# Gated SSM and squared-ReLU layer, forward and backward, on one core: the first dense layer by feature blocks ahead of the periods, its results loaded back and squared by ScalarE

## The chip, the core and the metric

The kernel runs on one core of a Trainium2 chip. Its engines are named as the profile names them: PE (TensorE matmul, with PEld for its weight loads), DVE (VectorE), ACT (ScalarE), POOL (GpSimd) and SP (SyncE). ACT, POOL and SP also issue transfers; a wait ahead of an issue is shown as SPq, ACTq or POOLq. Each engine works through its own instructions in the order in which they stand in the program, and semaphores hold an instruction until what it reads or overwrites is ready. The metric is the device time of one execution in microseconds (us).

## What is computed

The reference is the value and the gradients of one function. Cut to what matters here:

```
g = sigmoid((x * gate_w).sum(-1))
a = irfft(rfft(u) * rfft(K)) + u * Dskip          # K from A, B, C, log_dt (448 features, 256 states)
h = x @ w1 + b1                                   # 2048 x 448 @ 448 x 1792
r = where(h > 0, h, 0)
b = (r * r) @ w2 + b2                             # 1792 -> 448
out = g * a + (1 - g) * b
_out, _vjp = jax.vjp(f, ...); _grads = _vjp(grad_out)
```

The backward pass of the dense part needs r again: the gradient at h is 2 * r * (db @ w2.T), and the gradients of w1 and w2 read that product and the square of r. In both kernels r is therefore also written to memory (tensor `rT_d`, feature-major, 1792 x 2048).

## The kernel before, in words

The program has five parts, one after the other.

1. Start: loads, the gate, a first transform (`fwd1`) and transposes; `UT` (in tile `S25`, the variable `SB`) receives the transposed input, which is the moving operand of the first dense layer.
2. FFT stage: `powers` (a chain of squarings that ACT and DVE hand to each other, DVE L592 and L593, ACT L582 and L591), `spectra` (`load_s1`, `fwd2`), `products` (DVE L288) and `inv1` (PE L303), whose result goes to memory as `hd`. In parts 1 and 2 a scheduler decides the order of each engine's instructions from the dependencies; from part 3 on (`tc.manual_schedule()`) they stand as written.
3. Handover: `hd` is loaded back by SP (L312). DVE builds the tables of chunk 0 and then of chunk 1 (`tables`, `tables_y`), ACT first spreading each chunk's record over the table fields (`fields_x`, `fields_y`, L709 to L720). PE sums the convolution's rows with 116 matmuls (L1037); ACT copies the six results out (L1044); they go to memory (`dk_d`) and come back as `DK`; ACT copies transposed tables (L790), scales (L796), and copies out the first kernel chunk (L760).
4. Thirteen periods, one per chunk c = 1 to 13. The string `PERIOD` lists the tokens of a period; each builds the tables of chunk c and works backward on chunk c - 1. Ten of its tokens are `D`: at each, `D_` runs some steps of the generator `dense()`, so that the dense layers are spread evenly over the periods. The copy L760 stands near the end of each period and marks it in a trace.
5. Tail: the remaining rows of chunk 13, the second transform back, the parameter gradients, and the gradients of w1 and w2 (`units`, called by `Fl`).

The dense part before: `first_layer` goes through four token blocks (lb) of 512 and, in each, seven feature pairs (jp) of 2 x 128. One such step, an **h step** in what follows, is eight PE matmuls of 512 columns (six of 128 rows at L905, two of 64 rows at L908), two Relu on ACT out of two PSUM banks (L912), a write of r to memory by POOL (L913), and one square on DVE (L915, two steps late by `later`) into `hblk`. After the seven steps of a block `project` multiplies `hblk` with w2 in eight half steps (PE L883, ACT copy L887). At the last block the transposes of w1 (`turn_w1`, ACT copy L941) stand beside it, then those of w2 (`turn_w2`, L951). `second_layer` follows: per step matmuls, two scalings on ACT (L968) and one product with r, loaded back, on DVE (L971). Period 1 takes 8 of the 127 steps (`first_steps`), each later period 119/12. The square and the product are the dense part's only work on DVE.

All of w1 is loaded by SP in the handover (L1020, L1022). r has four buffers by turns (`rx`). The tables of chunks up to 6 are turned by four transposing transfers on SP (`load_yt`, L779); from chunk 7 on (`ON_PE`) the fourth is done by PE with two ACT copies (L790, R<-psN).

## Time and profile before

| | |
|---|---|
| runs | 805.06, 808.89 and 812.79 us, median 808.89 |
| the profiled execution's own time | 813.03 us |
| its span, first to last instruction | 811.2 us |
| busy PE / DVE / ACT / POOL | 621.9 / 612.7 / 539.4 / 162.0 us |
| granted TensorE clock, mean | 0.871 |
| end of each period (start of L760) | 257.9, 285.7, 311.0, 338.4, 363.9, 392.7, 418.8, 442.5, 469.6, 494.5, 519.7, 546.0, 568.7 us |
| start of period 1 (L760 of chunk 0) | 229.6 us |

Busy times overlap: they are shares of one span. A row of the windows view gives, for a stretch of the span, the busy time of each engine with the number of instructions, then the granted clock (1.00 is full speed), the DMA share and GB/s. A row of the timeline gives start, duration, engine, line, what it writes and reads, and in brackets how long the engine had sat idle and for whom it waited. Rows of the grouped lines end with the total busy time, the mean of one in ns, and the idle time before it.

### The profile page before, as it was taken

What the parts mean: (1) busy time and instruction counts of PE and PEld (TensorE: products, weight loads), DVE (VectorE), ACT (ScalarE), POOL (GpSimd) and SP (SyncE); (2) the same over time, 40 slices, a digit from 0 to 9 for tenths busy, and PEclk for the clock granted to TensorE, in tenths of its full rate; (3) what the DMA queues carried; (4) which work ended last, traced back from release to release, by engine and by line L of the source; (5) the groups of instructions that cost most, each with busy time, mean ns of one, the idle gap of its engine ahead of it and who ended that gap; (6) DMA issues with size and microseconds to landing.
All of it is one profiled execution on the core that took longest, in us unless ns stands there. A gap on an engine that the chain in (4) does not pass through costs nothing. (4 is left out here: it accounts for less than half of the span.)

```text
span 811.2 us, 17087 instructions
## 1 busy us (share of the span) xinstructions
PE 621.9 (77%) x6845; PEld 303.0 (37%) x6845; DVE 612.7 (76%) x947; ACT 539.4 (66%) x879; POOL 162.0 (20%) x264
## 2 busy tenths in 40 slices
PE   3776367663378889988989889989778689898985
PEld 1222122121243334434554444534535234444442
DVE  3795597877834999989789989989657864888263
ACT  0696467670578687968899879884575487465463
POOL 1222000042111132213231001101135311123122
PEclk9986555565688989999989999999989899999998
DMA  9978766279759387968986979895689998999972
GB/s 192 240 204 282 298 244 233 90 286 212 211 109 186 76 198 142 200 124 217 196 158 112 290 175 228 176 246 139 207 274 311 368 294 289 285 301 330 255 218 63
DMA packets 167214, 175.73 MB, mean 217 GB/s; under 512 B 104068, under 2 KB 144990, under 8 KB 166542
## 3 DMA queue, kind: packets, MB, share of 16 engines
q1 hardware_dynamic: 140152, 97.89, 49.9%
q0 software_dynamic: 17552, 56.44, 22.8%
q10 hardware_dynamic: 9430, 20.31, 7.2%
q8 instruction: 53, 0.87, 0.5%
q14 instruction: 27, 0.22, 0.1%
HBM read 83.67 MB, written 67.53 MB: 186 GB/s over the span
## 5 line engine op out<-in xcount | busy, mean ns | idle before, releaser
L817 ACT CAST P<-psF 128x1024 bf16<-128x1024 f32 x56 | 57.2, 1021 | 27.8 <-PE psF L815 27.7
L656 DVE TENSOR_TENSOR F<-X,F 128x1024 bf16<-128x1024 bf16 (+2 forms) x42 | 64.4, 1533 | 9.8 <-ACT X L689 7.3
L883 PEld LDWEIGHTS <-U 128*128 128x128 bf16 x448 | 40.9, 100 | 48.0 <-issue 16.6
L883 PE MATMUL psN<-D,U 128*128 128x448 bf16 x224 | 54.1, 386 | 1.1 <-DMA D<-in_B_w_dram 0.7
L888 POOL DMA_DIRECT2D br_d<-D x32 | 17.5, 548 | 180.0 <-ACT D L887 173.7
L1201 PEld LDWEIGHTS <-S 128*128 128x128 bf16 x416 | 39.0, 99 | 38.6 <-issue 9.3
L1201 PE MATMUL psX<-D,S 128*128 128x449 bf16 x224 | 47.2, 353 | 1.7 <-ACT S L1207 1.5
L883 PE MATMUL psN<-S,U 128*128 128x448 bf16 x224 | 46.8, 353 | 1.5 <-issue 1.3
L963 PE MATMUL psN<-S,K 128*128 128x512 bf16 x168 | 42.4, 386 | 6.0 <-ACT R L790 5.6
L815 PE MATMUL psF<-R,S 41*32 41x256 bf16 x896 | 24.7, 291 | 28.0 <-DVE P L828 17.4
L827 DVE TENSOR_TENSOR M<-P,psF 128x2048 bf16<-128x2048 bf16 x28 | 34.1, 1216 | 14.0 <-PE psF L773 12.5
L905 PE MATMUL psN<-S,K 128*128 128x512 bf16 x168 | 43.1, 395 | 0.0
L1201 PE MATMUL psX<-K,S 128*128 128x448 bf16 x192 | 41.2, 359 | 1.7 <-ACT S L1204 1.7
L1192 ACT ACTIVATE S<-psN 128x1024 bf16<-128x1024 bf16 x32 | 33.0, 1030 | 13.7 <-PE psN L1188 13.6
L303 PE MATMUL psN<-D,cb_MI 64*128 64x448 bf16 x96 | 31.7, 532 | 9.1 <-DVE D L288 5.5
L303 PEld LDWEIGHTS <-cb_MI 64*128 64x128 bf16 x256 | 17.6, 110 | 53.2 <-issue 46.5
L265 PEld LDWEIGHTS <-M 128*64 128x64 bf16 x192 | 13.9, 133 | 62.6 <-issue 54.9
L657 DVE TENSOR_TENSOR X<-F 128x512 bf16<-128x512 bf16 (+2 forms) x42 | 35.6, 847 | 1.4
L968 ACT ACTIVATE U<-psN 128x512 bf16<-128x512 f32 x56 | 31.1, 616 | 7.6 <-PE psN L966 5.3
L796 ACT COPY S<-K 128x128 bf16<-128x128 bf16 x56 | 34.9, 1007 | 0.0
L828 DVE TENSOR_TENSOR P<-P,psF 128x2048 bf16<-128x2048 bf16 x28 | 34.2, 1221 | 1.0
L773 PE MATMUL psF<-ident,X 128*128 128x128 bf16 x448 | 31.8, 228 | 3.0 <-ACT P L817 2.9
(350 smaller groups left out, 1617.3 us busy)
## 6 DMA issues: line engine op xcount, KB each, us to landing
sp<-K ACTq DMA_DIRECT2D x8, 896.0 KB
dhT_d<-U SPq DMA_DIRECT2D x28, 256.0 KB
R<-sp SPq DMA_DIRECT2D x8, 896.0 KB
S<-dhT_d POOLq DMA_DIRECT2D x14, 512.0 KB, 7.3
R<-hd SPq DMA_DIRECT2D x16, 448.0 KB
S<-rT_d POOLq DMA_DIRECT2D x12, 512.0 KB, 7.0
hd<-st SPq DMA_DIRECT2D x13, 448.0 KB
rec<-rec_d POOLq DMA_DIRECT2D x11, 448.0 KB, 4.8
```

Of the source, the lines that this page charges most:

```text
L303: nc.tensor.matmul(ps[kk2][:, 0:D], lhsT=MI[r0:r0 + 64, m, :], rhs=rh[r0:r0 + 64], start=(k_ == 0), stop=(k_ == len(terms) - 1), tile_posi ...
L656: V.tensor_tensor(out=Vt[:, 0:2 * w * n], in0=run(lo, 0, [0, 2], [NA, w], [1, n]), in1=run(PX[:, 0:1], 512 * k, [2, w], [0, n], [1, 2]), o ...
L657: V.tensor_tensor(out=run(lo, n, [NA * X2, 2], [NA, X2], [1, n]), in0=run(vb, 0, [n * X2, 2], [n, X2], [1, n]), in1=run(vb, (w + X2) * n, ...
L796: S.copy(D2[:, :, 0, 4 * l:4 * l + 4].rearrange("p (g i) a -> p a g i", g=NG), DK[:, l::4].rearrange("p a (e g q i) -> p a e q g i", g=NG, ...
L817: S.copy(zbs[c, g // 2][:, :, g % 2].rearrange("p t h k n -> p t k h n"), psz[:].rearrange("p t (k h n) -> p t k h n", k=2, h=2))
L827: V.tensor_tensor(out=pr.rearrange("p t g h k n -> p t (g h k n)"), in0=zv, in1=xv, op=ALU.mult)
L828: V.tensor_tensor(out=zv, in0=zv, in1=rev_dim(xv, 1), op=ALU.mult)
L883: T_.matmul(ps[:, 0:D], lhsT=hblk[:, j, P * tt:P * tt + P], rhs=ws[:, j, :], start=(w == 1 and j == 0), stop=(j == FT - 1))
L905: T_.matmul(pss[k][:], lhsT=w1w[:, dt, j * P:j * P + P], rhs=UT[:, dt, 512 * lb:512 * lb + 512], start=(dt == 0), stop=False, skip_group_c ...
L963: T_.matmul(pss[k][:], lhsT=w2Tw[:, jp, dt, k], rhs=dblk[:, dt], start=(dt == 0), stop=False, skip_group_check=True)
L1192: S.activation(hn(i)[:, 8 * th:8 * th + 8, :], ps[:], ACT.Square if i < FT else ACT.Copy)
L1201: T_.matmul(ps[:, 0:w], lhsT=hn(i)[:, t, :], rhs=(DB2[:, t, :] if i < FT else U[:, t, 0:w]), start=(t == 0), stop=(t == LT - 1))
```

## The change

The 28 h steps are now taken feature pair by feature pair (jp outer, lb inner), and only the 256 columns of w1 that a pair needs are loaded (`load_w1b`, seven blocks, the first five on POOL in the FFT stage, two on SP in the handover). 16 h steps (pairs 0 to 3) stand in the FFT stage, with one Relu on ACT and one on DVE; 4 (pair 4) in the handover and 8 (pairs 5 and 6) in period 1, with both on ACT. In the FFT stage and the handover they use the two PSUM banks X and S. r is only written to memory. Its buffers are four in the FFT stage, three in the handover, and from `del hbuf[2:]` on two.

Whole w1, for its transposes, is loaded after period 1 (`behind`), and r is loaded back by SP into six buffers (`load_rx`) and squared by ACT (`square`), blocks by turns into `hvs[0]` and `hblkB`, where the lower half of `KW` serves as the second buffer after w1. The seven `turn_w1` and the squares of block 1 stand in the first projection; the squares of blocks 2 and 3 in the next two. `ON_PE` begins at chunk 2. DVE has no squares any more. Periods 2 to 13 take the remaining 102 of 111 steps.

```diff
+    HP = FT // 2
+    W1B = ct["Ew_tile"]
+    w1bs = [RA[:, 7168:8192], SB[:, 11264:12288], Pct_[:, 7168:8192], RA[:, 7168:8192], Pct_[:, 7168:8192], W1B[:, 4096:5120], W1B[:, 5120:6144]]
+    def load_w1b(jp, q_):
+        wb, f0 = w1bs[jp], 256 * jp
+        q_.dma_start(wb[:, 0:3], bass.AP(tensor=B_w1.tensor, offset=B_w1.offset + f0, ap=[[F, P], [P * F, 3], [1, 256]]))
...
+    hleft = [(jp, lb) for jp in range(HP) for lb in range(4)]
+    hbuf = [RA[:, 10752 + 1024 * i:11776 + 1024 * i] for i in range(3)] + [Fp[:, 7168:8192]]
+    hbanks = [lambda: K.ps("X", [P, 512]), lambda: K.ps("S", [P, 512])]
+    def h_step(bks, on_act):
+        jp, lb = hleft.pop(0)
...
+        for k in range(2):
+            b1 = b1_f[:, 2 * jp + k:2 * jp + k + 1]
+            if on_act[k]:
+                S.activation(r[:, 512 * k:512 * k + 512], pss[k][:], ACT.Relu, bias=b1)
+            else:
+                V.tensor_scalar(out=r[:, 512 * k:512 * k + 512], in0=pss[k][:], scalar1=b1, scalar2=0.0, op0=ALU.add, op1=ALU.max)
+        G_.dma_start(pair_rows(rT_d, jp, lb), r.rearrange("p (k l) -> p k l", k=2))
+    def H(n=1):
+        for _ in range(n):
+            h_step(hbanks, (True, False))
     for q in range(4):
         if q < 3:
             spectra(q + 1)
+        if q == 0:
+            for jp in range(3):
+                load_w1b(jp, G_)
...
+        H(2)
         for h in range(2):
             K.products(Pct[:, h], spw[:, 2 * (q % 2) + 1, 2 * h:2 * h + 2], spw[:, 2 * (q % 2), 2 * h:2 * h + 2])
             K.inv1(None, q, hd[0], (h,), Pct[:, h])
+            H(1)
...
+    def load_rx(i, q):
+        if i < 4 * HP:
+            q.dma_start(rx[i % 6].rearrange("p (k l) -> p k l", k=2), pair_rows(rT_d, i % HP, i // HP))
+    def square(i):
+        jp, lb = i % HP, i // HP
+        hb = hblkB if lb % 2 else hvs[0][:, 0:7168].rearrange("p (j l) -> p j l", j=FT)
+        S.activation(hb[:, 2 * jp:2 * jp + 2].rearrange("p k l -> p (k l)"), rx[i % 6], ACT.Square)
+        load_rx(i + 6, nc.sync)
     def first_layer():
-                def sq(jp=jp, r=r):
-                    V.tensor_tensor(out=hblk[:, 2 * jp:2 * jp + 2].rearrange("p k l -> p (k l)"), in0=r, in1=r, op=ALU.mult)
-                later(sq)
...
+        while hleft:
+            h_step([bank, bank], (True, True))
+            yield
...
+        rx.extend([SB[:, 6272 + 1024 * i:7296 + 1024 * i] for i in range(4)] + [hv[:, 7168:8192], st4])
+        for i in range(6):
+            behind.append(lambda i=i: load_rx(i, nc.sync))
+        behind.append(lambda: nc.sync.dma_start(w1w[:, 0:3], bass.AP(tensor=B_w1.tensor, offset=B_w1.offset, ap=[[F, P], [P * F, 3], [1, F]])))
...
+        for i in range(HP):
+            square(i)
+            if i % 2:
                 yield
+        def ex0(k):
+            for v in (2 * k, 2 * k + 1):
+                if v < HP:
+                    turn_w1(v)
+                elif 8 <= v < 8 + HP:
+                    square(HP + v - 8)
+        yield from project(0, 0, w2n, ex0)
+        for lb in (1, 2):
+            yield from project(lb, 0, w2n, lambda k, lb=lb: square(HP * lb + HP + k) if k < HP else None)
...
     tables_y(0)
-    nc.sync.dma_start(w1w[:, 0:3], bass.AP(tensor=B_w1.tensor, offset=B_w1.offset, ap=[[F, P], [P * F, 3], [1, F]]))
...
     tables_y(1)
+    del hbuf[:]
+    hbuf += [SB[:, 8192:9216], SB[:, 9216:10240], SB[:, 11264:12288]]
+    for _ in range(4):
+        h_step(hbanks, (True, True))
     psS = [K.ps(NT[i], [P, 512]) for i in range(4)]
...
+    del hbuf[2:]
...
-    ON_PE = range(7, NCH - 1)
+    ON_PE = range(2, NCH - 1)
```

The order of the instructions at the places that matter, engine by engine (names with a line of the program, the operation, what it writes and reads, and the size; M and F are the record of chunk 1 and the table fields, psX and psS the two banks, U the constant weights of the row sums, S the tile `S25`).

ACT in the handover, before, from the last field of chunk 0 to the copies of the row sums:

```order
L720 ACTIVATE F_181_1339<-rec_1343 128x6x64x2 x2
L709 COPY F_181_1339<-M_182_1340 128x2x3x128
L712 ACTIVATE F_181_1339<-M_182_1340 128x3x128 x2
L717 COPY F_181_1339<-M_182_1340 128x6x256
L720 ACTIVATE F_181_1339<-M_182_1340 128x6x64x2 x2
L1044 CAST st_1532<-psN_184_1411 128x448
```

The same place now:

```order
L773 ACTIVATE F_213_1562<-rec_1566 128x6x64x2 x2
L762 COPY F_213_1562<-M_214_1563 128x2x3x128
L765 ACTIVATE F_213_1562<-M_214_1563 128x3x128 x2
L770 COPY F_213_1562<-M_214_1563 128x6x256
L773 ACTIVATE F_213_1562<-M_214_1563 128x6x64x2 x2
L652 ACTIVATE S_8_163<-psX_1637,b_f 128x512
L652 ACTIVATE S_8_163<-psS_1638,b_f 128x512
L652 ACTIVATE S_8_163<-psX_1650,b_f 128x512
L652 ACTIVATE S_8_163<-psS_1651,b_f 128x512
```

The eight Relu of the four handover steps (four are shown) stand behind the fields of chunk 1 and ahead of the copies of the row sums.

PE at that place, before: the last matmul of the FFT stage is followed by the row sums.

```order
L303 LDWEIGHTS cb_MI
L303 MATMUL psN_175_1312<-D_89_656,cb_MI 128x448
L1037 LDWEIGHTS U_90_657
L1037 MATMUL psN_184_1411<-D_89_656,U_90_657 32x448
L1037 LDWEIGHTS U_90_657
```

Now, from the end of the fourth handover step:

```order
L643 MATMUL psS_1677<-S_8_163,D_89_656 128x512
L646 LDWEIGHTS D_89_656
L646 MATMUL psX_1676<-S_8_163,D_89_656 128x512
L646 LDWEIGHTS D_89_656
L646 MATMUL psS_1677<-S_8_163,D_89_656 128x512
L1123 LDWEIGHTS U_90_657
L1123 MATMUL psN_224_1689<-D_89_656,U_90_657 32x448
```

All four h steps stand ahead of the first row sum, and each takes banks X and S again.

SP from the record of chunk 1 to the transposing transfers of chunk 2, before:

```order
L701 DMA M_182_1340<-rec_d 128x1792
L1020 DMA K_177_1325<-in_B_w_dram 128x3x1792
L1022 DMA K_177_1325<-in_B_w_dram 64x1792 x2
L701 DMA rec_1639<-rec_d 128x1792
L779 DMA_TRANSPOSE R_178_1328<-R_178_1328 128x16x128 x4
L1159 DMA cb_F1BD<-c_F1K 128x256
L779 DMA_TRANSPOSE R_178_1328<-Y_179_1329 128x16x128 x4
```

And now, from the record of chunk 2 on:

```order
L754 DMA rec_1916<-rec_d 128x1792
L832 DMA_TRANSPOSE R_210_1551<-R_210_1551 128x16x128 x4
L963 DMA S_8_163<-rT_d 128x2x512 x4
L963 DMA U_269_2428<-rT_d 128x2x512
L963 DMA st_1834<-rT_d 128x2x512
L982 DMA K_209_1548<-in_B_w_dram 128x3x1792
L984 DMA K_209_1548<-in_B_w_dram 64x1792 x2
L963 DMA S_8_163<-rT_d 128x2x512 x4
```

The load of whole w1 (L982, L984) has moved behind the six first loads of r (L963), and each later load of r stands behind the square that frees its buffer.

More of the change, by code (lines that the diff above doesn't have):

```diff
@@ L871, in later, with project @@
             lates.pop(0)()
-    def project(lb, w, ws):
+    hvs = []
+    def project(lb, w, ws, extra=None):
+        hb = hblkB if w == 0 and lb % 2 else hvs[0][:, 0:7168].rearrange("p (j l) -> p j l", j=FT)
         for tt in range(4):
@@ L882, in project @@
             for j in range(FT):
[L883 removed]
+                T_.matmul(ps[:, 0:D], lhsT=hb[:, j, P * tt:P * tt + P], rhs=ws[:, j, :], start=(w == 1 and j == 0), stop=(j == FT - 1))
                 if j == HP - 1:
+                    if extra:
+                        extra(2 * tt)
                     yield
+            held[0] = None
             br = brr[t % 4]
@@ L984 @@
     steps = dense()
-    done, total = 0, 4 * 2 * (HP + 8) + HP
+    first_steps = len(hleft) - 4 + 1
+    done, total = 0, first_steps + 3 + 4 * 8 + HP + 4 * (HP + 8)
     def D_(want):
@@ L1015 @@
     load_rec(1)
+    for jp in (5, 6):
+        load_w1b(jp, nc.sync)
     tables(0)
```

89 lines of the change are left out of this document (49 added, 40 removed).

## The prediction

> **What bounds the kernel now.** I read the windows first, cut where the program's parts end: FFT stage, handover, period 1, periods 2 to 3, 4 to 6, 7 to 13.
>
> ```profile
> core 0: us, PE busy (x) PEld busy (x) DVE busy (x) ACT busy (x) POOL busy (x), PEclk, DMA share, GB/s
> 89.00:181.00 92.00, 60.21 (x240) 20.60 (x239) 75.44 (x152) 62.19 (x125) 9.23 (x8) 0.57 0.57 213
> 181.00:229.59 48.59, 19.34 (x308) 11.54 (x308) 34.31 (x39) 20.08 (x28) 9.61 (x10) 0.61 0.75 195
> 229.59:257.86 28.27, 22.06 (x308) 9.55 (x309) 8.76 (x11) 21.67 (x34) 5.42 (x7) 0.87 0.92 180
> 257.86:310.97 53.11, 46.81 (x649) 21.18 (x649) 50.28 (x59) 38.01 (x58) 11.22 (x18) 0.87 0.68 132
> 310.97:392.65 81.68, 74.53 (x1065) 36.34 (x1064) 73.87 (x86) 63.88 (x98) 20.24 (x32) 0.96 0.84 175
> 392.65:568.69 176.04, 155.30 (x2444) 81.42 (x2441) 163.35 (x185) 143.28 (x217) 27.22 (x47) 0.97 0.83 191
> ```
>
> No single engine bounds the whole. In periods 2 to 13 DVE is busy for 90 to 95% of each stretch: there it sets the pace, with PE close behind. In the FFT stage DVE has 82%, at a granted PE clock of 0.57. In the handover every engine idles most of the time, so a chain of waits sets its length, and in period 1 DVE has only 8.76 us of 28.27. The change takes work from DVE and PE where they are full and puts it where they are not. The question is whether the moved steps are really free there.
>
> The handover's chain stands in ACT's timeline:
>
> ```profile
> 205.53 0.83 ACT L709 COPY F<-M 128x768 bf16<-128x768 bf16 x1 [21.36 <-DMA M<-rec_d]
> 208.47 1.57 ACT L720 ACTIVATE F<-M 128x768 bf16<-128x768 bf16 x2
> 209.95 0.51 ACT L1044 CAST st<-psN 128x448 bf16<-128x448 f32 x1
> 219.50 1.01 ACT L790 COPY R<-psX 128x1024 bf16<-128x1024 bf16 x1 [4.65 <-POOL P L1060]
> 220.41 1.02 ACT L790 COPY R<-psS 128x1024 bf16<-128x1024 bf16 x1
> 229.59 0.76 ACT L760 CAST P<-psX 128x328 bf16<-128x328 f32 x1
> 234.20 1.27 ACT L912 ACTIVATE S<-psN,b_f 128x512 bf16<-128x512 f32 x2 [1.90 <-PE psN L908]
> ```
>
> ACT waits 21.36 us for the record of chunk 1, spreads it, copies the row sums at 209.95, and all behind that, by way of memory, ends 19.64 us later at L760. Two back-to-back ACT copies of 1024 start 0.91 us apart, two Relu of 512 take 1.27. PE's timeline at the same place, and its first h steps in period 1:
>
> ```profile
> 196.20 0.96 PE L1037 MATMUL psN<-D,U 128*32 128x448 bf16 x8 [2.10 <-DMA D<-hd]
> ...
> 198.04 0.61 PE L1037 MATMUL psF<-D,U 128*32 128x448 bf16 x4
> ...
> 207.34 0.54 PE L1037 MATMUL psF<-P,U 128*32 128x448 bf16 x3
> ...
> 231.15 2.69 PE L905 MATMUL psN<-S,K 128*128 128x512 bf16 x6
> ...
> 234.44 1.47 PE L905 MATMUL psN<-S,K 128*128 128x512 bf16 x6
> 235.84 0.39 PE L908 MATMUL psN<-S,K 64*128 64x512 bf16 x2
> ```
>
> The row sums are finished at 207.88, before ACT can copy them. The 24 from 196.20 to 198.65 took 0.10 us each. An h step's matmuls take 1.47 plus 0.39, with a little overlap 1.8 us; at the low clock the six alone take 2.69, so about 3.3 with the last two.
>
> **The change, part by part.** The sum is made against the profiled execution (813.03 us, 4.14 above the median).
>
> FFT stage, 16 steps. Each adds one Relu on ACT (1.27 / 2 = 0.64), one on DVE, and PE 1.8 to 3.3 us. For DVE's read from PSUM the nearest row is:
>
> ```profile
> L219 DVE CAST K<-psN 128x448 bf16<-128x448 f32 x22 | 13.4, 622 | 19.0 <-PE psN L265 18.8
> ```
>
> So DVE gets 16 x 0.62 = 10 us in 92 that are 75.44 full, ACT 10 us, PE 29 to 53 us in 92 that are 60.21 full. At its present density DVE's 10 us would cost 10 / 0.82 = 12; put wholly into its 16.6 idle us, nothing; if PE stays at the low clock, 60 + 53 - 92 = 21. A gain isn't excluded (rival two): -6 to +21. I take +9, nearest to DVE's share, since the two banks are single and each step's Relu stand in line on both engines. The writes of r (16 of 256 KB) fall in a stage with a DMA share of 0.57: nothing, as long as the four buffers cover a landing. The seven blocks of w1, three issues each, stand on POOL (9.23 us busy of 92) and, two of them, on SP ahead of the record of chunk 2, which nothing reads before period 1: nothing.
>
> Handover, 4 steps. PE can do the first step while it waits for `hd`, but the second needs banks X and S, and their Relu stand on ACT behind the fields of chunk 1, so behind the 21.36 us wait. From the end of the fields (209.95, later by what the FFT stage adds) PE has three steps to go, each ending in a Relu: 1.8 + 0.7 = 2.5 us, at the low clock 3.3 + 0.7 = 4.0, together 7.5 to 12. Only then come the 116 row sums, which until now were done before: 116 x 0.10 = 11.8 us, or half of it at twice the clock, 5.9. So the copies at 209.95 move by 13 to 24 us, and the 19.64 us behind them move along. I take 10.5 + 6.5 = +17: steps mostly at the low clock because PE pauses for each Relu, row sums mostly at the high one because nothing interrupts them. The load of whole w1, which goes, was queued behind the record, so its going brings little.
>
> Period 1. Before, 7 h steps with four buffers; now 8 with two, so that a step's Relu wait for the write of r two steps earlier to land. POOL's timeline and the transfers of period 1:
>
> ```profile
> 237.83 0.73 POOL L913 DMA_DIRECT2D rT_d<-S  x1 [1.31 <-ACT S L912]
> ...
> 241.40 1.10 POOL L1152 DMA_DIRECT2D D<-in_B_w_dram  x1
> 242.49 0.71 POOL L913 DMA_DIRECT2D rT_d<-st  x1
> ...
> 258.27 0.71 POOL L913 DMA_DIRECT2D rT_d<-U  x1 [6.05 <-ACT U L912]
> ```
>
> ```profile
> D<-in_B_w_dram POOLq DMA_DIRECT2D x1, 1568.0 KB, 12.3
> rT_d<-S POOLq DMA_DIRECT2D x4, 256.0 KB, 6.8
> rT_d<-U POOLq DMA_DIRECT2D x2, 256.0 KB, 3.6
> rT_d<-st POOLq DMA_DIRECT2D x1, 256.0 KB, 12.4
> ```
>
> The write behind the load of w2 (L1152) took 12.4 us, others 3.6 to 6.8. The even steps make a chain: the second is written at 237.83; the fourth's Relu end 6.8 + 1.3 later; its write lies behind w2, 12.4 + 1.3; the sixth to the eighth again 8.1. That is 267.7, against 258.27 for the last write before: +9. With landings of 3.6 it is +3; with none in the way 0; with two slow ones +14. Behind these Relu on ACT stand the copies and fields of the period, which PE and DVE wait for. The projection's half step that leaves period 1 (about 1.3 us of PE) is paid for by the eighth h step.
>
> Periods 2 and 3. DVE loses its squares, ACT gets them. The squares and ACT's parts:
>
> ```profile
> 257.86:310.97 53.11, 6.01 (x10) 0.87 0.68 132
> 310.97:392.65 81.68, 9.28 (x14) 0.96 0.84 175
> ```
>
> ```profile
> 257.86:310.97 53.11, 9.33 (x15) 0.87 0.68 132
> 310.97:392.65 81.68, 18.37 (x28) 0.96 0.84 175
> ```
>
> ```profile
> L790 ACT COPY R<-psN 128x1024 bf16<-128x1024 bf16 x16 | 17.6, 1164 | 1.1 <-PE psN L789 1.1
> L887 ACT CAST D<-psN 128x448 bf16<-128x448 f32 x32 | 17.5, 546 | 23.1 <-PE psN L883 22.9
> L951 ACT COPY K<-psN 128x1024 bf16<-128x1024 bf16 x7 | 7.2, 1066 | 0.3 <-PE psN L950 0.3
> L941 ACT COPY S<-psN 128x896 bf16<-128x896 bf16 x7 | 6.4, 910 | 4.5 <-PE psN L940 4.4
> ```
>
> The first pair is DVE's L915 (the squares) in these stretches, the second ACT's L912 (Relu). Without the Relu and six copies L887, ACT keeps 38.0 - 9.3 - 3.3 = 25.4 us. The new order puts into these two periods 20 squares (0.91 each by the copies above, 18.2), seven `turn_w1` copies (6.4), seven L887 (3.8) and four L790 of `ON_PE` (4.7): 58.5 us in a stretch of 53.11. ACT becomes the bound here. The fullest it ever was in a period:
>
> ```profile
> 392.65:418.81 26.16, 23.34 (x405) 14.35 (x403) 22.90 (x25) 24.43 (x34) 8.03 (x13) 0.87 0.78 170
> ```
>
> is 24.43 of 26.16, 93%; so 58.5 / 0.93 = 63, +10.
>
> Periods 4 to 6: DVE keeps 73.87 - 9.28 = 64.6 us, at its 0.904 there 71.5, -10. ACT: 63.9 less Relu 18.4, nine L887 (4.9) and five L941 (4.6) is 36.0; eight squares, nine L887, seven L951 and six L790 bring 26.8, so 62.8, below DVE. PE only loses here. On SP the loads of r stand ahead of the next period's transposing transfers and wait for squares; those transfers wait for DVE's tables anyway, which are later than the squares: nothing. Periods 7 to 13 keep their products on DVE (28, as before): 0. The tail: 0.
>
> Sum: 9 + 17 + 9 + 10 - 10 = +35, so 848 for a profiled execution, and 808.89 + 35 = **844** for the median.
>
> **Rivals.** One, faster: the idle time holds the 24 moved steps. Then FFT stage, handover and period 1 cost nothing, and periods 2 to 6 fall to DVE's 50.28 + 73.87 - 6.01 - 9.28 = 108.9 us at 0.928 (periods 7 to 13), 117.3 instead of 134.8: -17.5, so 791. For it speak DVE's 16.6 and ACT's 29.8 idle us in the FFT stage; against it that the moved Relu stand behind ACT's wait. It decides if the moved steps cost below 9 us together, ACT included. 0.07.
>
> Two, the clock: the steps fill PE in the FFT stage, the clock comes up from 0.57, and the stage shrinks, since its own matmuls shorten and DVE and ACT wait less for them: -6 there instead of +9, and 13 in the handover: +16, so 825. For it: 0.87 in period 1 at 78% busy. Against it: at 65% busy it stood at 0.57, and each step pauses for two Relu. 0.18. The Trainium skill's page "TensorE: Matmul & The Clock Gate", Part 1, has this rule: the clock is halved until PE has been busy through a window of about 3.4 us, then full. By it the FFT stage would be paid back at least in part, and the sum would be rival two's 825; by the row of 0.57 at 60 us busy it is the 844 above.
>
> Three, late loads: period 2's first squares wait for loads that SP can issue only after the last writes of r have freed the same space, and PE's `turn_w1` waits for w1 behind them. Whole w1 is as large as w2, which took 12.3 us to land: +12 more, 856. For it: six loads of 256 KB ahead of w1. Against it: `turn_w1` comes some four D later. 0.20.
>
> **How the numbers follow.** Forecast 0.50 (844), rival two 0.18 (825), three 0.20 (856), one 0.07 (791), 0.05 for what I don't see. The terms' ends (-6 to 21, 13 to 24, 0 to 14, and some 5 either way in the periods), not all at one end, make about 20 either way: 822 to 864 holds the forecast and rivals two and three and leaves out rival one. About 1% is what a measurement can tell: faster (below 801) 0.07, within 1% 0.08, slower (above 817) 0.85.
>
> **What would show it.** In the profile after: the row sums (now L1123) end well after ACT's fields of chunk 1, and ACT waits for PE there; ACT waits for DMA ahead of the Relu in period 1; period 1 lasts some 37 us from one kernel copy (L760, now L813) to the next, periods 2 and 3 some 30 each with ACT above 90% busy, periods 4 to 6 some 24. Row sums that end before the fields, a period 1 under 30 us, or an FFT stage no longer than before would each prove a term wrong.

## The result, and the profile after

The changed kernel takes 896.45 us (median of four runs, 894.34 to 899.21) beside 810.12 for the kernel before on the same chip: a ratio of 1.108, 95% interval 1.101 to 1.114. The direction was forecast, the size was not: +86 us instead of +35, outside the range. The profiled execution took 894.34 us with a span of 892.6, so 81.4 more than the span of 811.2 before; that is the sum to explain. (In e4, e6, e8, e9 and e15 below the profiled execution was a disturbed one, with a period 1 of 46 to 56 us; its period 1 and its total are left out of every comparison, and ratios rest on undisturbed executions alone.)

The same windows, cut at the same events in the changed kernel (columns as before: length, then busy time of each engine, granted clock, DMA share, GB/s):

```profile
89.00:210.00 121.00, 90.30 (x353) 27.68 (x360) 85.79 (x167) 70.09 (x136) 25.93 (x30) 0.73 0.56 205
210.00:277.94 67.94, 25.89 (x347) 14.42 (x347) 34.60 (x40) 28.09 (x42) 12.51 (x16) 0.70 0.54 139
277.94:312.04 34.10, 21.24 (x332) 9.85 (x337) 6.15 (x7) 22.58 (x35) 6.15 (x8) 0.85 0.77 179
312.04:384.29 72.25, 48.22 (x705) 25.43 (x688) 47.58 (x53) 57.81 (x76) 7.23 (x13) 0.81 0.57 159
384.29:462.38 78.09, 60.14 (x1028) 34.17 (x1030) 64.26 (x69) 63.26 (x86) 8.09 (x15) 0.90 0.72 157
462.38:648.52 186.14, 144.91 (x2315) 73.22 (x2327) 162.21 (x184) 134.79 (x207) 20.65 (x37) 0.94 0.76 170
```

Busy times came out near the forecast: ACT 57.81 in periods 2 and 3 (forecast 58.5), DVE 64.26 in periods 4 to 6 (64.6), DVE 10.4 more in the FFT stage (10). The lengths did not, so the missing time is waiting. Three places show it. First the FFT stage. Two rows of its waits (total, times, longest), and the wait that follows in the handover; of DVE's two waits the longer lies in the stage, the other, 5.3 us, ends at 211.6, behind the last write of `hd`:

```profile
DVE F L654 <- DMA rT_d<-F: 12.7, 2, 7.4
PE psS L643 <- DVE F L654: 7.7, 2, 7.1
ACT F L762 <- DMA rT_d<-F: 7.6, 1, 7.6
```

The timelines of DVE, ACT and POOL give the story of one buffer of r, F (L654 is DVE's Relu, L652 ACT's, L655 the write):

```profile
144.79 0.74 DVE L654 TENSOR_SCALAR F<-psS,b_f 128x512 bf16<-128x512 f32 x1
...
170.94 0.67 ACT L652 ACTIVATE F<-psX,b_f 128x512 bf16<-128x512 f32 x1
...
172.52 0.72 POOL L655 DMA_DIRECT2D rT_d<-F  x1
...
179.12 0.75 DVE L654 TENSOR_SCALAR F<-psS,b_f 128x512 bf16<-128x512 f32 x1 [7.41 <-DMA rT_d<-F]
```

DVE fills its half at 144.79, ACT its half 26 us later, the write lands 6.6 us after it was issued, and DVE, whose order is fixed, has stood 7.41 us before the next Relu into F. In the handover, ACT's timeline:

```profile
234.30 0.83 ACT L762 COPY F<-M 128x768 bf16<-128x768 bf16 x1 [8.22 <-DMA M<-rec_d]
...
239.17 1.47 ACT L770 COPY F<-M 128x1536 bf16<-128x1536 bf16 x1 [3.20 <-DVE F L726]
...
242.02 0.67 ACT L652 ACTIVATE S<-psX,b_f 128x512 bf16<-128x512 f32 x1
...
253.25 0.68 ACT L652 ACTIVATE S<-psS,b_f 128x512 bf16<-128x512 f32 x1
258.44 0.53 ACT L1131 CAST st<-psN 128x448 bf16<-128x448 f32 x1 [4.51 <-PE psN L1123]
...
277.94 0.76 ACT L813 CAST P<-psX 128x328 bf16<-128x328 f32 x1
```

The eight Relu stand between the fields and the copies of the row sums, and the copies wait for PE: as forecast. The fields of chunk 1 end later as well, since one of them (L770) waits 3.20 us for DVE's tables of chunk 0, whose own fields had waited for the write of F. The waits of periods 1, then 2, then 3 and 4:

```profile
ACT S L652 <- DMA rT_d<-S: 8.5, 2, 6.9
```

```profile
ACT U L968 <- DMA S<-rT_d: 7.2, 2, 4.1
...
PE psN L1021 <- DMA K<-in_B_w_dram: 5.6, 2, 5.3
```

```profile
DVE M L880 <- PE psF L826: 19.4, 2, 11.1
...
PE psF L868 <- DMA R<-R: 10.1, 2, 9.7
PE psF L868 <- DMA R<-Y: 7.2, 1, 7.2
```

Period 1 waits for landings of r; period 2 for loads of r (L968 is the square) and of whole w1 (L1021 is in `turn_w1`): rival three's late loads. In periods 3 and 4 PE's `back_z` (L868) waits for the transposing transfers, and DVE behind PE.

### The profile page after: what moved, and what is told of

Its sections match the earlier page's. It is cut to its first block, busy times and chain, and to the rows that moved or that the text cites. A ratio compares the mean times of both kernels' runs of the same rounds, so it can differ in the third digit from the quotient of the medians.

```text
span 892.6 us, 17327 instructions
## 1 busy us (share of the span) xinstructions
PE 636.3 (71%) x6899; PEld 308.6 (35%) x6925; DVE 607.6 (68%) x935; ACT 567.0 (64%) x901; POOL 163.3 (18%) x268
## 3 DMA queue, kind: packets, MB, share of 16 engines
q0 software_dynamic: 17184, 54.35, 19.7%
## 5 line engine op out<-in xcount | busy, mean ns | idle before, releaser
L880 DVE TENSOR_TENSOR M<-P,psF 128x2048 bf16<-128x2048 bf16 x28 | 34.1, 1217 | 54.9 <-PE psF L826 42.5
L868 PE MATMUL psF<-R,S 41*32 41x256 bf16 x896 | 25.8, 303 | 61.7 <-DVE P L881 19.0
L940 PE MATMUL psN<-S,U 128*128 128x448 bf16 x224 | 51.7, 374 | 5.5 <-DVE U L1053 5.4
L1045 PE MATMUL psN<-S,K 128*128 128x512 bf16 x154 | 42.0, 395 | 6.7 <-ACT R L843 5.2
L940 PEld LDWEIGHTS <-U 128*128 128x128 bf16 x336 | 31.3, 103 | 44.1 <-issue 13.9
L1050 ACT ACTIVATE U<-psN 128x512 bf16<-128x512 f32 x56 | 31.3, 615 | 10.1 <-PE psN L1048 10.0
L868 PEld LDWEIGHTS <-S 41*32 41x32 bf16 x896 | 9.5, 91 | 79.6 <-issue 40.3
L881 DVE TENSOR_TENSOR P<-P,psF 128x2048 bf16<-128x2048 bf16 x28 | 34.2, 1221 | 1.0
L826 PEld LDWEIGHTS <-X 128*128 128x128 bf16 x448 | 29.0, 103 | 15.9 <-issue 14.6
L219 DVE CAST K<-psN 128x448 bf16<-128x448 f32 x22 | 13.4, 621 | 26.7 <-PE psN L265 26.4
L303 PE MATMUL psN<-D,cb_MI 64*128 64x448 bf16 x96 | 28.6, 444 | 4.0 <-DVE D L288 2.9
L303 PEld LDWEIGHTS <-cb_MI 64*128 64x128 bf16 x256 | 16.7, 100 | 40.9 <-issue 34.2
```

Of the source, the lines that this page charges most:

```text
L303: nc.tensor.matmul(ps[kk2][:, 0:D], lhsT=MI[r0:r0 + 64, m, :], rhs=rh[r0:r0 + 64], start=(k_ == 0), stop=(k_ == len(terms) - 1), tile_posi ...
L826: T_.transpose(ps[:, t, 128 * b:128 * b + 128], Xs[c % 2][:, o_:o_ + 128], ident[:])
L868: T_.matmul(psz[32 * ii:32 * ii + 32, t, 256 * k:256 * k + 256], lhsT=DKc[64 * t:64 * t + NY, c % 2, CW * g + i].rearrange("p s a -> p (s ...
L880: V.tensor_tensor(out=pr.rearrange("p t g h k n -> p t (g h k n)"), in0=zv, in1=xv, op=ALU.mult)
L881: V.tensor_tensor(out=zv, in0=zv, in1=rev_dim(xv, 1), op=ALU.mult)
L940: T_.matmul(ps[:, 0:D], lhsT=hb[:, j, P * tt:P * tt + P], rhs=ws[:, j, :], start=(w == 1 and j == 0), stop=(j == FT - 1))
```

## The experiments

Stage times are read from ACT's timeline: the last write of `hd` (end of the FFT stage), the first copy of the row sums, the first kernel copy (k_out of chunk 0), and the sums of periods between kernel copies. "Median" takes all executions of a kernel, "ratio" is its time to that of the kernel before on the same chip. A dash stands for one of the five long periods named above.

| kernel | median us | ratio, 95% | last hd | row sums | k_out 0 | P1 | P2-3 | P4-6 | P7-13 |
|---|---|---|---|---|---|---|---|---|---|
| before | 810.12 | 1 | 180.4 | 210.0 | 229.6 | 28.3 | 53.1 | 81.7 | 176.0 |
| the change | 896.45 | 1.108, 1.101 to 1.114 | 208.9 | 258.4 | 277.9 | 34.1 | 72.2 | 78.1 | 186.1 |
| e1_fft_none | 871.00 | 1.073, 1.070 to 1.077 | 183.6 | 229.0 | 248.6 | 36.2 | 72.0 | 81.5 | 185.3 |
| e2_fft_bufs | 888.48 | 1.094, 1.089 to 1.099 | 199.9 | 243.6 | 263.2 | 36.2 | 74.1 | 79.5 | 188.4 |
| e3_hand | 894.81 | 1.102, 1.098 to 1.106 | 213.0 | 246.5 | 278.0 | 37.0 | 72.8 | 82.3 | 182.8 |
| e4_spacing | 901.24 | 1.108, 1.103 to 1.112 | 212.5 | 264.1 | 283.5 | - | 59.6 | 86.8 | 184.6 |
| e5_p1 | 898.33 | 1.104, 1.096 to 1.112 | 210.4 | 262.8 | 282.3 | 26.0 | 77.8 | 80.9 | 182.8 |
| e6_rxpool | 885.14 | 1.090, 1.082 to 1.097 | 211.3 | 263.0 | 282.4 | - | 65.4 | 74.5 | 190.8 |
| e7_sqdve | 892.32 | 1.100, 1.093 to 1.107 | 212.3 | 259.7 | 279.2 | 36.7 | 66.8 | 78.1 | 189.4 |
| e8_act_both | 886.86 | 1.091, 1.083 to 1.099 | 203.7 | 248.4 | 267.9 | - | 75.7 | 80.0 | 190.5 |
| e9_spfree | 881.21 | 1.085, 1.079 to 1.092 | 211.5 | 263.2 | 282.6 | - | 64.2 | 71.7 | 179.9 |
| e10_quarter | 878.77 | 1.082, 1.076 to 1.088 | 197.0 | 241.9 | 261.4 | 36.2 | 71.9 | 80.3 | 181.3 |
| e11_hand2 | 887.79 | 1.095, 1.088 to 1.103 | 210.7 | 244.1 | 263.2 | 35.2 | 73.6 | 78.0 | 186.6 |
| e12_all | 844.25 | 1.041, 1.035 to 1.047 | 200.1 | 233.5 | 253.0 | 28.4 | 65.4 | 74.5 | 178.1 |
| e13_short | 894.85 | 1.099, 1.091 to 1.107 | 206.3 | 252.6 | 271.9 | 34.2 | 71.7 | 78.0 | 186.2 |
| e14_all_sqdve | 843.17 | 1.032, 1.024 to 1.041 | 201.4 | 234.4 | 253.7 | 27.5 | 62.1 | 74.5 | 177.6 |
| e15_short_quarter | 888.40 | 1.090, 1.080 to 1.099 | 193.3 | 239.5 | 259.0 | - | 72.3 | 81.6 | 186.6 |

Stages with the same code differ by 2 to 5 us from one kernel to another (periods 7 to 13 more, 181 to 191), so a stage counts only beyond that. The last hd write, for one, comes at 208.9 to 213.0 in the eight kernels with the change's FFT stage.

### The FFT stage: e1_fft_none, e2_fft_bufs

```diff
-            h_step(hbanks, (True, False))
+            jp, lb = hleft.pop(0)
+            G_.dma_start(pair_rows(rT_d, jp, lb), UT[:, 0, 0:1024].rearrange("p (k l) -> p k l", k=2))
```

> The sixteen first-layer steps of the FFT stage are left out: no matmuls and no Relu, and the write of each step takes its 256 KB from a constant tile, so nothing is held for it (the first layer's values of feature blocks 0 to 3 are then not those of the reference; everything else is computed). The trace after has the last hd write at 208.86 us where before had 180.40, 28.5 later, and chunk 0's fields 3.6 us later still. If the steps' work or their buffers make these 32 us, the kernel gets 26 to 34 us shorter, 862 to 870, and the last hd write is back at 178 to 184. If only the loads and writes of the steps slow the stage (they stay here), it stays within 8 us of 896.

The time fell by 3.4% of the kernel before, to 871, and the last hd write came at 183.63: inside the expectation for the write, 1 us beyond it for the time. Loads of w1's blocks and writes, which stay, are worth 3.2 us at most, no more than stages vary by; the steps with their buffers make 25.2 us of the 28.5.

```diff
-    hbuf = [RA[...] for i in range(3)] + [Fp[:, 7168:8192]]
+    hbuf = [RA[...] for i in range(3)] + [W1B[:, 6144 + 1024 * i:7168 + 1024 * i] for i in range(2)]
```

> Five buffers for r in the FFT stage instead of four: the fourth, which lies in the tile that chunk 0's fields use, is replaced by two 1024-column pieces of the free end of another tile. Theory of the held buffer: a step's DVE half fills its half of a buffer early, its ACT half comes some 26 us later, the write lands 6.5 to 7.5 us after that, and DVE stands before the next Relu into that buffer (12.7 us in two waits, with ACT and PE behind it), and chunk 0's fields wait 7.6 us for the last write. With five buffers and the shared tile free: the two waits of DVE go or shrink to a third and the fields' wait goes, together 10 to 22 us, 874 to 886. Rival, the added work itself (16 Relu on each of two engines and PE's slow matmuls in a stage with no slack): only the fields' wait goes, 890 to 894, and the last hd write stays within 4 us of 208.86.

The held buffer is shown, as part of it: the last hd write came 8.9 us earlier (199.9 to 201.4 in the three kernels that have just this stage, against 208.9 to 213.0), and the row sums follow it after 43.7 us instead of 49.6: neither chunk 0's fields nor L770 wait any more. The time, 888.48, lies between the two forecasts. These 14.8 us at the first kernel copy became 1.3% of the whole, about 11 us by the ratios; some came back in later periods. What is left of the stage, 16.3 us over e1_fft_none, is little want of buffers: DVE's waits for writes of r in the stage come to 3.2 us now.

### What is left of the FFT stage: e8_act_both, e10_quarter, e13_short, e15_short_quarter

All four have the five buffers. In e8_act_both `H` calls `h_step(hbanks, (True, True))`.

> Against the run with five buffers (888.5 us, last hd write at 199.92 us): both halves of each step of the FFT stage are taken by ACT, none by DVE, five buffers as there. DVE has 16 reads from PSUM fewer (about 10 us), ACT 16 more. Theory of the halves that stand far apart: a bank and a buffer are now held for one Relu after the other, the last hd write comes at 184 to 194, and the time is 873 to 883. Theory of the full engines: DVE has 82% of this stage before the change and ACT 68%, so taking 10 us off DVE helps as well, but by at most these 10 us; if ACT's queue is what the stage stands on, the last hd write is as late as 199 or later and the time 888 or more.

In this profile the last hd write came 3.8 us later than with a half on each engine, no more than stages vary by, and the ratios, 1.091 and 1.094, are the same. DVE lost 9 us of busy time (86.6 to 77.2) and ACT gained 10, and nothing was won: with five buffers the runs show no price of the distance between the halves, nor of DVE's share.

```diff
-            for dt in range(DT - 1):
-                T_.matmul(..., start=(dt == 0), stop=False, ...)
+            for dt in range(1 if jp < 4 else DT - 1):
+                T_.matmul(..., start=(dt == 0), stop=(jp < 4), ...)
...
-        for k in range(2):
+        for k in range(2 if jp > 3 else 0):
```

> Against the run with five buffers (888.5 us, last hd write at 199.92): in the sixteen steps of the FFT stage only one of a half's four matmuls is left (a quarter of the sum over the model dimension, so their r is not the first layer's); Relu, buffers and writes are as there. If PE's work at the low clock is what the 16 to 20 us left in the stage are, the last hd write comes at 183 to 190 and the time falls by 9 to 16, 872 to 880. If it is the Relu on DVE and ACT (10 us each, and the standing in line for two single banks), the last hd write stays at 195 or later and the time within 5 us of 888.

The last hd write came at 196.97, so three quarters of the matmuls are worth 3.0 us, within what stages vary by, and the rival is nearer. The time fell by 1.2%, more than the stage: periods 7 to 13 were 7 us shorter, though no code there differs.

```diff
+            n = 64 if jp < 4 else 512
-                S.activation(r[:, 512 * k:512 * k + 512], pss[k][:], ACT.Relu, bias=b1)
+                S.activation(r[:, 512 * k:512 * k + n], pss[k][:, 0:n], ACT.Relu, bias=b1)
```

> Against the run with five buffers (last hd write at 199.92 us): in the sixteen steps of the FFT stage each Relu takes 64 of its 512 columns (the rest of the buffer is zero, so their r is not the first layer's); matmuls, writes, banks and order are as there, and the five buffers are cleared by POOL once beforehand. If the busy time of the Relu on DVE and ACT (10 us on each) is what is left in the stage, the last hd write comes at 184 to 191. If the place of the steps in the engines' orders is (each Relu waits for its matmuls, these for the bank, and the FFT's own work stands behind), it stays at 195 or later.

The last hd write came later, at 206.34: not to be read as a price of the Relu. This stage's order is the scheduler's, and with shorter Relu it came out another. ACT's timeline of this run at the end of the stage:

```profile
200.60 0.84 ACT L765 COPY F<-rec 128x768 bf16<-128x768 bf16 x1
...
202.36 1.47 ACT L773 COPY F<-rec 128x1536 bf16<-128x1536 bf16 x1
202.90 0.37 ACTq L307 DMA_DIRECT2D hd<-st  x1
...
203.93 1.02 ACT L218 CAST S<-psN 128x448 bf16<-128x448 f32 x2
```

Chunk 0's fields stand ahead of the last casts of the stage. Inconclusive by itself; the two edits together:

> The last two together: one of four matmuls a half and Relu of 64 columns in the sixteen steps of the FFT stage, five buffers. Hardly any work is left, but all the waits between the engines. If work is what costs, the last hd write is back at 182 to 188, within 5 us of the run without the steps (183.63); if the order is, at 193 or later.

193.29, at the border of "the order costs": with a quarter of the matmuls and an eighth of the Relu's columns the stage is still 9.7 us longer than without the steps. The windows of the FFT stage, from 89 us to its end, in e1_fft_none, e15_short_quarter, e10_quarter and e2_fft_bufs:

```profile
89.00:184.00 95.00, 60.26 (x247) 20.56 (x249) 74.13 (x149) 61.98 (x124) 14.56 (x19) 0.59 0.63 238
```

```profile
89.00:194.00 105.00, 76.90 (x270) 22.97 (x272) 78.22 (x168) 66.20 (x139) 24.36 (x29) 0.61 0.63 235
```

```profile
89.00:197.00 108.00, 79.48 (x272) 23.89 (x272) 86.09 (x168) 70.16 (x138) 26.14 (x31) 0.58 0.62 230
```

```profile
89.00:200.00 111.00, 86.70 (x353) 27.57 (x360) 86.55 (x168) 70.10 (x137) 25.18 (x29) 0.77 0.60 220
```

So the 28.5 us are, from 180.40 on: loads and writes 3.2 (to 183.63), the presence of the steps 9.7 (193.29), the length of the Relu 3.7 (196.97), the other matmuls 3.0 (199.92), too few buffers 8.9 (208.86). The terms of 3 to 4 us are each no larger than what stages vary by, so only the buffers, the 9.7 and the sum of the rest count. The order may move with each edit too. The traces show it: DVE's 53 casts and products of the FFT (L219, L230, L288) stand in one order in the change and, but for a cast or two, in e2_fft_bufs and e10_quarter; in the kernel before, e1_fft_none, e13_short and e15_short_quarter more of them have moved. So of the 9.7, what the 32 remaining matmuls make (PE is 16.6 us busier than without them), what waiting in line makes and what another order of the FFT's own work makes is not told apart.

### The handover: e3_hand, e11_hand2

e3_hand moves the four `h_step` calls behind the loads of the row sums, ahead of `Pt = K.t("P14", ...)`.

> The four steps of the handover are put behind the row sums, their copies and the loads that read them back, so that neither PE's steps nor ACT's eight Relu stand ahead of the row sums. Theory of the prediction (row sums wait for three steps that each end in a Relu behind ACT's fields): the copies of the row sums follow the fields within 3 us again and period 1 begins 13 to 17 us earlier, of which up to 4 are given back as ACT and PE do the steps later: 880 to 886. Rival: the handover is late because chunk 0's and chunk 1's tables are late, and the steps only fill that time: within 5 us of 896.

Row sums follow the last hd write after 33.5 us instead of 49.6, so they did wait for the steps; but the kernel copy is where it was (277.99; counted from the last hd write, 65.0 us instead of 69.1). ACT's timeline there:

```profile
246.49 0.51 ACT L1128 CAST st<-psN 128x448 bf16<-128x448 f32 x1
...
254.46 0.69 ACT L652 ACTIVATE S<-psX,b_f 128x512 bf16<-128x512 f32 x1 [3.07 <-DMA K<-dk_d]
...
265.71 0.68 ACT L652 ACTIVATE S<-psS,b_f 128x512 bf16<-128x512 f32 x1
...
268.35 1.01 ACT L843 COPY R<-psX 128x1024 bf16<-128x1024 bf16 x1 [1.96 <-POOL P L1147]
...
277.99 0.78 ACT L813 CAST P<-psX 128x328 bf16<-128x328 f32 x1
```

The steps now stand ahead of the eight copies of `turn_y` (L843) on ACT: the same 12 us, at another place of the same chain. The time agrees with "no change" though the mechanism is the forecast one.

e11_hand2 moves them the other way, ahead of the fields of chunk 1:

```diff
     tables(0)
+    del hbuf[:]
+    hbuf += [SB[:, 8192:9216], SB[:, 9216:10240], SB[:, 11264:12288]]
+    for _ in range(4):
+        h_step(hbanks, (True, True))
     fields_x(0)
```

> The four steps of the handover are put ahead of chunk 1's fields in the program, so that on ACT their Relu stand ahead of the 21 us wait for the record of chunk 1 instead of behind it; they get the same buffers and banks. Theory of the prediction (what costs there is the place of the Relu on ACT, not their work): the row sums follow the fields at once and nothing is put behind them, so the first kernel copy comes 12 to 18 us earlier than 277.9 and the time is 878 to 885. Rival: PE's and ACT's work of the steps costs the handover as much at this place too (they delay chunk 1's fields or its tables): within 5 us of 896.

ACT's timeline of this run:

```profile
228.07 0.67 ACT L652 ACTIVATE S<-psX,b_f 128x512 bf16<-128x512 f32 x1
...
237.88 0.68 ACT L652 ACTIVATE S<-psS,b_f 128x512 bf16<-128x512 f32 x1
238.45 0.83 ACT L762 COPY F<-M 128x768 bf16<-128x768 bf16 x1
...
244.07 0.51 ACT L1131 CAST st<-psN 128x448 bf16<-128x448 f32 x1
```

The Relu fill the wait for the record, the fields start without a wait, and the row sums come 33.4 us after the last hd write: 16.2 less than after the change, and the kernel copy 14.7 earlier, as the theory has it. In the whole time it is 1.2%, 887.79 and so between the two forecasts (the intervals overlap a little).

### Period 1: e5_p1

```diff
-    del hbuf[2:]
+    hbuf[2:] = [W1B[:, 6144:7168], W1B[:, 7168:8192]]
```

> Four buffers for r in period 1 instead of two (two pieces of a tile's free end are added). Theory of the prediction (two buffers, and a write that lies behind the load of w2 in its queue, make ACT wait 8.5 us for landings): period 1, 34.1 us in the trace after, falls to 28 to 30, and the time to 889 to 893. Rival: the same wait comes again in period 2, whose loads of r wait for the last writes: period 2 gets longer by what period 1 gains, and the time stays within 3 us of 896.

Period 1 fell to 25.97 us and ACT's wait for landings there is gone, but period 2 rose from 37.87 to 43.73 and the time stayed: the rival. The waits of period 2 in this run:

```profile
ACT U L968 <- DMA rT_d<-U: 5.8, 1, 5.8
...
ACT U L968 <- DMA S<-rT_d: 4.9, 1, 4.9
...
PE psN L1021 <- DMA K<-in_B_w_dram: 4.2, 2, 3.7
```

What period 1 gains, period 2 spends waiting for the last writes, for r and for w1.

### Periods 2 to 13: e6_rxpool, e9_spfree, e7_sqdve, e4_spacing

```diff
-        load_rx(i + 6, nc.sync)
+        load_rx(i + 6, G_)
...
-            behind.append(lambda i=i: load_rx(i, nc.sync))
+            behind.append(lambda i=i: load_rx(i, G_))
```

> The loads of r for the squares are issued by POOL instead of SP. Theory of the late transfers: on SP they wait for squares, and the transposing transfers of the next period stand behind them, so that PE waits for those (17 us in periods 3 and 4) and DVE for PE; with SP free of them, periods 2 to 6 (150 us together) get 8 to 15 us shorter, 881 to 888. Rival: the transfers are late for another reason (DVE's tables, or the landing itself), and POOL's queue, which also writes the projection's rows, takes over the waiting: periods 2 to 6 within 4 us of 150.

Periods 2 to 6 fell from 150.3 to 139.9, where the ten kernels with the change's code in these periods, itself included, have 150 to 159, and the time by 1.8% of the kernel before: SP's order is a cause. SP's timeline of the changed kernel in periods 3 and 4 (L963 loads r, L832 is a transposing transfer; a long row is a queue that stood):

```profile
361.57 9.41 SPq L963 DMA_DIRECT2D S<-rT_d  x4
...
383.06 1.74 SPq L963 DMA_DIRECT2D S<-rT_d  x2
384.89 8.78 SPq L832 DMA_TRANSPOSE R<-R  x3
393.76 6.50 SPq L963 DMA_DIRECT2D S<-rT_d  x2
```

and what SP waited for there:

```profile
SPq L963 <- ACT U L968: 15.7, 5, 5.8
SPq L963 <- ACT K L968: 8.9, 3, 5.5
```

24.6 us of waiting for squares, with the transposing transfers at 384.89 behind them. Periods 7 to 13 did not gain; SP's timeline of e6_rxpool ahead of period 7 shows another such wait:

```profile
456.50 16.67 SPq L957 DMA_DIRECT2D D<-rT_d  x6
473.27 11.07 SPq L832 DMA_TRANSPOSE R<-Y  x3
```

Six loads of r for the second layer, which the change had moved to SP too, stand 16.67 us for PE's `turn_w2` (14.04 us in the change itself, so this is no new cost of e6_rxpool). e9_spfree puts these on POOL as well:

```diff
-                load_r(k + 1, nc.sync)
+                load_r(k + 1)
```

> Beside the loads of r for the squares, the loads of r and of the gradient for the second layer that the change had moved from POOL to SP are back on POOL; SP is left with the transposing transfers and what it had before. Theory of SP's order: in periods 7 and 8 these loads wait on SP for PE's transposes of w2 (15.9 us in six waits in the run with only the first loads moved) and the transposing transfers stand behind them; periods 7 and 8, 54.5 us after the change and 62 in that run, fall to 48 to 52, and the whole to 872 to 880. Rival: those transfers wait for DVE's tables and copies anyway, so periods 7 and 8 stay at 54 or more and the time at 882 to 888.

SP's transfers ahead of period 7 in this run:

```profile
443.21 9.21 SPq L832 DMA_TRANSPOSE R<-R  x3
465.30 12.01 SPq L832 DMA_TRANSPOSE R<-Y  x3
```

Nothing stands ahead of them now. Periods 7 and 8 took 50.7 us (54.5 after the change, 49.9 before), periods 4 to 6 71.7, the forecast's 71.5. Periods 7 to 13, 179.9, lie below the 181 to 191 of all kernels with these loads on SP, and so do those of the two kernels further down that also have them on POOL (178.1 and 177.6). In the whole time it is 0.5% beside e6_rxpool, within the intervals, and 881.21 is just beyond the forecast: the profiles show it, the whole time hardly.

```diff
-        S.activation(hb[...], rx[i % 6], ACT.Square)
+        V.tensor_tensor(out=hb[...], in0=rx[i % 6], in1=rx[i % 6], op=ALU.mult)
```

> The 28 squares are done by DVE from the loaded r (one product each) instead of by ACT; all else stays. Theory of the prediction (ACT is the bound in periods 2 and 3, since it has 20 squares there): these two periods, 72.2 us in the trace after, fall to 60 to 67, and periods 4 to 6, where DVE sets the pace, grow by 3 to 6. Rival (loads of r and w1 and the transposing transfers are late, ACT merely stands behind them): periods 2 and 3 stay at 70 to 76. The whole: 886 to 893 by the theory, 894 to 904 by the rival.

Periods 2 and 3 fell to 66.8, at the edge of the theory, and periods 4 to 6 did not rise; the time is 0.8% lower with overlapping intervals. The squares' place on ACT is some 5 of the 19 us there, little beyond what stages vary by; the late loads and SP's order are more.

```diff
-first_steps + (total - first_steps) * ((c - 2) * nd + k) // (nd * (NCH - 2))
+first_steps + spread(119 * ((c - 2) * nd + k) // (nd * (NCH - 2)))
...
+    def spread(x):
+        n1 = 3 + 4 * 8 + HP
+        return n1 * x // 59 if x < 59 else n1 + x - 59
```

> Only the spacing of the dense layer's steps in periods 2 to 13 is changed: the first layer's 42 left steps go over the same stretch of periods as the first layer had before (59 of 119 parts), and the second layer's 60 steps fall where they fell in the kernel before. Theory of alignment: in periods 7 to 13, which got 10 us longer though DVE, ACT and PE are each less busy than before, the projection stands in PE's order right behind products that DVE has late in its order; with the old places these periods take 176 to 180 instead of 186, and periods 2 to 6 get shorter by up to 8 since ACT's squares are thinner: 880 to 890. Rival, the order of the transposing transfers and of the eighths of the Toeplitz operand moved to PE and ACT costs the time: periods 7 to 13 stay at 184 or more and the time within 5 us of 896.

The time did not move: the theory that the places in the period alone cost the 10 us of periods 7 to 13 fell. Squares spread thinner did shorten periods 2 and 3 by 12.6, and periods 4 to 6 got 8.7 longer: moved, not saved. Periods 9 to 13 took 127.1, as before (126.2; after the change 131.7), but period 8 took 32.8 (25.9 after the change).

### All together: e12_all, e14_all_sqdve

e12_all holds the edits of e2, e11, e5, e9 and e4, and has SP load whole w1 in period 1, at the place where POOL loads w2:

```diff
                 G_.dma_start(w2n, ...)
+                nc.sync.dma_start(w1w[:, 0:3], ...)
+                for h in range(2):
+                    nc.sync.dma_start(w1w[64 * h:64 * h + 64, 3], ...)
```

> All of these together: five buffers in the FFT stage, the handover's steps ahead of chunk 1's fields, four buffers in period 1, the loads of r and of the gradient on POOL, the second layer's steps at the places that they had before, and whole w1 loaded for its transposes during period 1 instead of behind six loads of r in period 2. If the costs found are separate they add up: 8 in the FFT stage, 12 to 18 in the handover, 10 to 15 in periods 2 to 6, 5 to 10 in periods 7 to 13, 4 to 6 for w1: 840 to 860, still above the kernel before, since 16 to 20 us of the FFT stage and the squares on ACT stay. If they hide one another: 865 to 880.

The costs add up, as expected: 844.25, 5.8% below the change and still 4.1% above the kernel before. By the ratios the mends won 4.8% of the kernel before when made singly (e2 1.3, e11 1.2, e9 2.3, e5 and e4 nothing clear of the intervals) and 6.7% together. Part of it is that period 1's gain stays now: periods 1 and 2 take 63.0 us together, 72.0 after the change and 69.7 in e5_p1. Why it stays, and what the earlier load of w1 does by itself, was not run. Its windows of the FFT stage, periods 2 and 3, 4 to 6, 7 to 13:

```profile
89.00:200.13 111.13, 87.07 (x360) 27.57 (x360) 86.43 (x168) 70.22 (x137) 25.14 (x29) 0.77 0.60 219
...
281.43:346.79 65.36, 44.34 (x691) 25.79 (x683) 46.67 (x52) 53.67 (x70) 21.19 (x32) 0.78 0.71 168
346.79:421.30 74.51, 59.82 (x957) 32.25 (x956) 63.46 (x68) 61.22 (x84) 15.71 (x27) 0.87 0.59 130
421.30:599.43 178.13, 153.73 (x2407) 80.41 (x2406) 163.89 (x186) 141.15 (x215) 26.75 (x46) 0.94 0.82 188
```

Against before: FFT stage +19.7, handover +3.7, periods 2 and 3 +12.3, 4 to 6 -7.2, 7 to 13 +2.1, the rest +1.3; 31.9 of span.

> Against the version with all mends (844.25 us; periods 2 and 3 65.4 us, 4 to 6 74.5): the squares are done by DVE. If ACT is what periods 2 and 3 still stand on, they fall to 56 to 61 and periods 4 to 6 rise by 2 to 6, the time is 838 to 843. If the loads of r and w1 or PE's added transposes are, periods 2 and 3 stay at 64 to 67 and the time at 844 to 850.

Periods 2 and 3: 62.1, between the two; the time is the same as e12_all's. Squares on ACT are at most some 3 of the 12 us that were left, no more than stages vary by; the cause of the other 9 stays open. No version made here beats the kernel before.

## Why the prediction was wrong

Term by term, predicted and then measured between the profiled spans:

- **FFT stage, +9, measured +28.5: the step that failed.** "I take +9, nearest to DVE's share" and "nothing, as long as the four buffers cover a landing". DVE's share was right as work (85.79 busy us instead of 75.44), and most of the Relu's columns with three quarters of the matmuls are worth 6.7 us by the experiments. Two costs were missing. Buffers (8.9): I compared four buffers with a landing, but a buffer is held from the first half's Relu to the landing of the second half's write, 34 us in the rows above, because the halves stand far apart in the orders of DVE and ACT. And 12.9 us that remain with hardly any work in the steps: 3.2 with the loads and writes alone, 9.7 more once the steps stand there. The sum divided work into idle time, and for standing in line it had only the choice of +9 between -6 and +21; the stage went beyond that upper end. That an inserted step delays what stands behind it, in a stage where each engine waits for another, is the likely reading of the 9.7, not a shown one.
- **Rival two's premise came true, its conclusion not.** The clock rose from 0.57 to 0.73, with five buffers to 0.77, and the stage got longer. The Trainium skill's page "TensorE: Matmul & The Clock Gate", Part 1, ties the full clock to PE staying busy. The trace agrees only in part: 0.77 at 86.70 busy us of 111, but 0.58 at 79.48 of 108 (e10_quarter). A higher clock, then, came without a shorter stage; what the clock alone is worth the two don't show, since the run at 0.77 has four times the matmuls in its steps.
- **Handover, +17, measured +19.9** from the last hd write to the kernel copy. Right in mechanism and nearly in size: from the end of chunk 1's fields (242.0) to the first copy of the row sums (258.44) it is 16.4 us, and e3_hand and e11_hand2 take 16 us away ahead of the row sums by moving the steps alone. The other 3.6 come ahead of that: chunk 0's fields waited 7.6 us for the write of the buffer that shares their tile, DVE's tables came late by it, and L770 stood 3.20 us for them; I had not looked for that overlap.
- **Period 1, +9, measured +5.8** (+6 to +9 in the eight kernels with two buffers and no dash in the table). Right in mechanism, but wrong as a term of a sum: with four buffers the time comes back in period 2 (e5_p1), since its loads wait for the same writes.
- **Periods 2 and 3, +10, measured +19.1.** ACT's busy time was right (57.81), but "ACT becomes the bound here" was not: it was busy for 80% of the 72.25 us, not 93%, and taking the squares off it won some 5 (e7_sqdve). The rest is waiting: rival three's late loads, which I gave 0.20 and 12 us, and SP's order: with the loads of r on POOL these periods fall to 65.4 (e6_rxpool).
- **Periods 4 to 6, -10, measured -3.6.** "On SP the loads of r stand ahead of the next period's transposing transfers and wait for squares; those transfers wait for DVE's tables anyway, which are later than the squares: nothing." Refuted: with those loads on POOL the periods take 74.5, with the second layer's loads there too 71.7, the -10 of the forecast. The sentence compared finish times of the kernel before, in which no squares stood on ACT.
- **Periods 7 to 13, 0, measured +10.1.** The sum took the periods as unchanged because their products are, and passed over the loads of r and of the gradient that the diff moves from POOL to SP. With these back, 179.9, 178.1 and 177.6 in three kernels; the rest is within what these periods vary by, 181 to 191 with the loads on SP, the spacing (184.6) included.

Rival one (the idle time holds the steps) is out: nowhere did moved steps come nearly free except e11_hand2's (52.6 us from the last hd write to the kernel copy, 49.2 before), which fill a wait that was named.

## What to carry to other kernels

Count a buffer's time from its first writer to the landing of its last write, by the two engines' orders, not by the transfer alone; and look up what else lies in its tile. When loads change queues, list for each what it waits for in the new kernel and what stands behind it there: an issue that waits blocks its queue like an instruction. Put filler work ahead of the wait it is to fill, in the order of the engine that waits; behind that wait the same work costs its full length.

## What the runs showed of the hardware

A write of 256 KB behind the 1568 KB load of w2 in POOL's queue had landings of very different length. After the change ACT's longest wait for one was 6.9 us; in five profiled executions of kernels with two buffers period 1 took 46 to 56 us, with single such waits of 14.0 to 25.9 us, in the eight others 34 to 37, and in the three kernels with four buffers 26.0 to 28.4. Why a landing takes so long at times is open.
